# A mixture-of-experts step on 32-column quarters of TensorE, with the hidden layer turned on VectorE

## The chip, the cores and the metric

The kernel runs on one core of a Trainium2 chip. The metric is the device time of one execution in microseconds (us), from the first to the last instruction. A core has five engines that run side by side: TensorE (PE) multiplies matrices, VectorE (DVE) and ScalarE (ACT) work elementwise, GpSimd (POOL) and SyncE (SP) here mostly start transfers between the chip's main memory and the core's own memory (SBUF). TensorE takes two operands from SBUF: one (`lhsT`, the stationary one) is loaded into its array first, the other (`rhs`, the moving one) streams through. The result lands in PSUM, whence ScalarE or VectorE fetch it.

## The reference: attention, a router, and one expert for each token

All is in float32. Attention within chunks of 64 positions gives 4608 token rows of 512 values. A router picks one of 8 experts for each row by cosine similarity. The expert is a two-layer network, 512 to 1024 to 512, whose result is scaled by the router's weight. Cut to what matters:

```python
# q, k, v: (8, 8, 576, 64); w1: (8, 512, 1024); w2: (8, 1024, 512)
x = chunk_attention(q, k, v)                  # (4608, 512), chunks of 64
logits = normalize(x) @ normalize(expert_emb).T / tau
expert_idx = np.argmax(logits, axis=1)
gate_w = softmax(logits)[np.arange(N), expert_idx]
for e in range(E):
    mask = expert_idx == e
    h = np.maximum(x[mask] @ w1[e], 0.0)      # first layer, ReLU
    out[mask] = gate_w[mask, None] * (h @ w2[e])   # second layer
```

## The kernel before

The kernel has two stages. The first computes attention and the router, writes the token rows to main memory and sorts them by expert into groups of up to 64 rows. The second takes two groups at a time, so 128 rows are one step (`j`), and each half of the step (`s`) has its own expert's weights. There are 37 steps. 36 of them (`LEAST`) are in a software pipeline; the last one stands alone behind a branch (`more`), since the number of steps depends on the data. The names are `P = 128`, `G = 64`, `D = 512`, `F = 1024`, `KD = D / P = 4`, `KF = F / P = 8`.

A step has these parts. `turn_xb` turns the step's 128 rows on TensorE (a product with the identity), so that the 512 inputs lie on the partitions. `gates` works out the router's weights on ScalarE and VectorE. `hidden` is the first layer, `turn_h` turns its result, and `result` is the second layer:

```python
def hidden(j):
    d = mo[j]
    h = bp.tile([P, F], FP32, tag="h", name="h")
    for fh in range(F // 512):
        ps = ps_h.tile([P, 512], FP32, tag="h", name="h_ps")
        for c in range(KD):
            for s in range(2):
                nc.tensor.matmul(
                    ps[G * s : G * s + G],
                    lhsT=d["xT"][:, c, G * s : G * s + G],
                    rhs=w1_sb[s][j % 2][:, c, fh * 512 : fh * 512 + 512],
                    start=(c == 0), stop=(c == KD - 1),
                )
        dst = h[:, fh * 512 : fh * 512 + 512]
        if fh % 2:
            nc.scalar.activation(dst, ps, AF.Relu)
        else:
            nc.vector.tensor_scalar(dst, ps, 0.0, None, ALU.max)
    d["h"] = h

def turn_h(j):
    d = mo[j]
    hT = bp.tile([P, KF, P], FP32, tag="hT", name="hT")      # two buffers
    for g in range(KF // 4):
        ps = ps_ht.tile([P, 4, P], FP32, tag="ht", name="ht_ps")
        for c in range(4):
            f0 = (4 * g + c) * P
            nc.tensor.transpose(ps[:, c], d["h"][:, f0 : f0 + P], ident)
        if g % 2:
            nc.scalar.copy(hT[:, 4 * g : 4 * g + 4], ps)
        else:
            nc.vector.tensor_copy(hT[:, 4 * g : 4 * g + 4], ps)
    d["hT"] = hT

def result(j):
    d = mo.pop(j)
    ps = ps_y.tile([P, D], FP32, tag="y", name="y_ps")
    for c in range(KF):
        for s in range(2):
            nc.tensor.matmul(
                ps[G * s : G * s + G],
                lhsT=d["hT"][:, c, G * s : G * s + G],
                rhs=w2_sb[s][j % 2][:, c],
                start=(c == 0), stop=(c == KF - 1),
            )
    y = bp.tile([P, D], FP32, tag="y", name="y", bufs=3)
    nc.scalar.activation(y, ps, AF.Copy, scale=d["gate"])
    # ... (the rows of y are sent to their places in the output)
```

A matmul whose result lies on 64 of the 128 partitions uses 64 of the array's 128 columns; the two halves `s` of a step use the two halves of the array in turn. The order of the parts in the loop:

```python
for j in range(LEAST + 1):
    if j + 1 < LEAST:
        hidden(j + 1)
        # ... load_w1(j + 3): weights, only where the expert changes
    if j < LEAST:
        turn_h(j)
    if j + 2 < LEAST:
        turn_xb(j + 2)
        gates(j + 2)
    if j > 0:
        result(j - 1)
        # ... load_w2(j + 1)
    # ... (rows for later steps are gathered)
# ... more(LEAST): the last step, its parts one after the other
```

In the first stage, the attention scores (`sc`) are also matmuls on parts of the array: tiles of 64 rows by 64 columns, four of them in turn, 16 matmuls for each 128 rows.

Of the kernel before, what the change touches and what calls it, by code (L numbers as in the profile page):

```python
# [9 lines left out]
FP32 = mybir.dt.float32  # L10
BF16 = mybir.dt.bfloat16
I32 = mybir.dt.int32
AF = mybir.ActivationFunctionType
ALU = mybir.AluOpType
AX = mybir.AxisListType
PSUM = bass.MemoryType.PSUM
ENG = mybir.EngineType

P = 128
# [6 lines left out]
def kernel(  # L26
# [11 lines left out]
    nc = tc.nc  # L38
    B, H, S, Dh = q.shape
    E, D = moe_expert_emb.shape  # L40
    F = moe_w1.shape[2]
    N = B * S
    NPAIR = H // 2
    KD = D // P
    KF = F // P
    NT = N // P
    NCB = S // CH
    G = P // 2
    NST = NT + E // 2
    scale = 1.0 / float(Dh) ** 0.5  # L50
    XBUF = 4
# [13 lines left out]
    w1_sb = [[keep.tile([P, KD, F], FP32, name=f"w1_{s}{i}") for i in range(2)] for s in range(2)]  # L65
    w2_sb = [[keep.tile([P, KF, D], FP32, name=f"w2_{s}0")] for s in range(2)]
    w1_rows = moe_w1.rearrange("e (c p) f -> p (e c) f", p=P)
    w2_rows = moe_w2.rearrange("e (c p) d -> p (e c) d", p=P)
    ident = keep.tile([P, P], FP32, name="ident")
# [492 lines left out]

    with (
        tc.tile_pool(name="blk", bufs=2) as bp,
        tc.tile_pool(name="ps_x", bufs=1, space=PSUM) as ps_x,
        tc.tile_pool(name="ps_h", bufs=3, space=PSUM) as ps_h,
        tc.tile_pool(name="ps_ht", bufs=2, space=PSUM) as ps_ht,
        tc.tile_pool(name="ps_y", bufs=2, space=PSUM) as ps_y,
    ):
        def number(ap, top, *engines):  # L570
            return nc.values_load(
                ap,
                engines=engines,
                min_val=0,
                max_val=top,
                skip_runtime_bounds_check_because="a count of comparisons, less than this",
            )

        new = {}

        def load_w(buf, rows, n, s, j):

            if (s, j) not in new:
                new[s, j] = (
                    number(eblk[G * s : G * s + 1, j : j + 1], E - 1, ENG.SP),
                    number(fresh[G * s : G * s + 1, j : j + 1], 1, ENG.SP),
                )
            e, f = new[s, j]
            nc.sync.dma_start(out=buf[s][j % 2], in_=rows[:, ds(e * n, n), :], cond=f > 0)

        def load_w1(j):
            for s in range(2):
                load_w(w1_sb, w1_rows, KD, s, j)

        def load_w2(j):
            for s in range(2):
                load_w(w2_sb, w2_rows, KF, s, j)
                del new[s, j]

        def turn_xb(j):  # L600
            t = xin.pop(j)
            ps = ps_x.tile([P, KD, P], FP32, tag="x", name="x_ps")
            for c in range(KD):
                nc.tensor.transpose(ps[:, c], t[:, c * P : c * P + P], ident)  # L604
            xT = bp.tile([P, KD, P], FP32, tag="xbT", name="xbT")
            nc.vector.tensor_copy(xT, ps)
            mo[j] = {"xT": xT, "xin": t}

        def gates(j):
            d = mo[j]  # L610
            x, lg = d["xin"], spot[:, j, 0:E]
            junk = bp.tile([P, D], FP32, tag="junk", name="junk", bufs=1)
            rn = bp.tile([P, 1], FP32, tag="rn", name="rn")
            lmax = bp.tile([P, 1], FP32, tag="lmax", name="lmax")
            sh = bp.tile([P, E], FP32, tag="sh", name="sh")
            gate = bp.tile([P, 1], FP32, tag="gate", name="gate", bufs=4)
            nc.scalar.activation(junk, x, AF.Square, accum_out=rn)
            nc.scalar.activation(rn, rn, AF.Sqrt)  # L618
            nc.vector.tensor_reduce(lmax, lg, axis=AX.X, op=ALU.max)
            nc.vector.tensor_scalar(rn, rn, 1e-6, None, ALU.add)  # L620
            nc.vector.reciprocal(rn, rn)
            nc.vector.tensor_scalar(sh, lg, lmax, rn, ALU.subtract, ALU.mult)
            nc.scalar.activation(sh, sh, AF.Exp, accum_out=gate)  # L623
            nc.vector.tensor_scalar(gate, gate, 1e-9, None, ALU.add)
            nc.vector.reciprocal(gate, gate)
            d["gate"] = gate

        def hidden(j):
            d = mo[j]
            h = bp.tile([P, F], FP32, tag="h", name="h")  # L630
            for fh in range(F // 512):
                ps = ps_h.tile([P, 512], FP32, tag="h", name="h_ps")
                for c in range(KD):
                    for s in range(2):
                        nc.tensor.matmul(  # L635
                            ps[G * s : G * s + G],
                            lhsT=d["xT"][:, c, G * s : G * s + G],
                            rhs=w1_sb[s][j % 2][:, c, fh * 512 : fh * 512 + 512],
                            start=(c == 0),
                            stop=(c == KD - 1),  # L640
                        )
                dst = h[:, fh * 512 : fh * 512 + 512]
                if fh % 2:
                    nc.scalar.activation(dst, ps, AF.Relu)  # L644
                else:
                    nc.vector.tensor_scalar(dst, ps, 0.0, None, ALU.max)  # L646
            d["h"] = h

        def turn_h(j):
            d = mo[j]  # L650
            hT = bp.tile([P, KF, P], FP32, tag="hT", name="hT")
            for g in range(KF // 4):
                ps = ps_ht.tile([P, 4, P], FP32, tag="ht", name="ht_ps")
                for c in range(4):
                    f0 = (4 * g + c) * P
                    nc.tensor.transpose(ps[:, c], d["h"][:, f0 : f0 + P], ident)  # L656
                if g % 2:
                    nc.scalar.copy(hT[:, 4 * g : 4 * g + 4], ps)
                else:
                    nc.vector.tensor_copy(hT[:, 4 * g : 4 * g + 4], ps)  # L660
            d["hT"] = hT

        def result(j):
            d = mo.pop(j)
            ps = ps_y.tile([P, D], FP32, tag="y", name="y_ps")
            for c in range(KF):
                for s in range(2):
                    nc.tensor.matmul(  # L668
                        ps[G * s : G * s + G],
                        lhsT=d["hT"][:, c, G * s : G * s + G],  # L670
                        rhs=w2_sb[s][j % 2][:, c],
                        start=(c == 0),
                        stop=(c == KF - 1),
                    )
            y = bp.tile([P, D], FP32, tag="y", name="y", bufs=3)
            nc.scalar.activation(y, ps, AF.Copy, scale=d["gate"])  # L676
            ins = nc.gpsimd.indirect_dma_start(  # L677
                out=out,
                out_offset=bass.IndirectOffsetOnAxis(ap=spot[:, j, E : E + 1].bitcast(I32), axis=0),
                in_=y,  # L680
                in_offset=None,
                bounds_check=N - 1,
                oob_is_err=False,
            )
            tc.declare_no_dep(ins.ins, group="rows", reason="blocks hold different tokens")
            tc.add_to_no_dep_group("rows", ins.ins)

        load_w1(0)
        load_w1(1)
        load_w2(0)  # L690
        load_w2(1)
        turn_xb(0)
        hidden(0)
        load_w1(2)
        gates(0)
        turn_xb(1)
        gates(1)

        LEAST = NT
        for j in range(LEAST + 1):  # L700
            if j + 1 < LEAST:
                hidden(j + 1)
                if j + 3 < NST:
                    load_w1(j + 3)
            if j < LEAST:
                turn_h(j)
            if j + 2 < LEAST:
                turn_xb(j + 2)
                gates(j + 2)
            if j > 0:  # L710
                result(j - 1)
                if j + 1 < NST:
                    load_w2(j + 1)
            if j + XBUF < NST:
                gather_x(j + XBUF)
                if j + XBUF + 1 < NST:
                    gather_spot(j + XBUF + 1)

        steps = number(n_steps, NST, ENG.PE, ENG.DVE, ENG.Activation, ENG.Pool, ENG.SP)

        def more(j):
            with tc.If(steps > j):
                turn_xb(j)
                hidden(j)
                if j + 2 < NST:
                    load_w1(j + 2)
                turn_h(j)
                gates(j)
                result(j)
                if j + 2 < NST:  # L730
                    load_w2(j + 2)
                if j + 1 < NST:
                    more(j + 1)

        more(LEAST)


# [26 lines left out]
```

## Time and profile before

| | before |
|---|---|
| median of 3 runs | 804.73 us (802.67 to 807.33) |
| profiled execution | 810.2 us |
| TensorE matmuls busy | 743.9 us (92%) |
| TensorE weight loads busy | 367.7 us (45%) |
| VectorE busy | 251.7 us (31%) |
| ScalarE busy | 290.7 us (36%) |
| mean of transfers | 163 GB/s |

In the profile a matmul instruction in float32 appears as two records, each with a record of a weight load (LDWEIGHTS) before it. A line of a group gives the line of the source, the engine, the operation, what it writes and reads, the part of the array (128\*64 is 128 rows by 64 columns), the shape and the number of records, then the busy time in us and the mean length of a record in ns, and last the engine's idle time ahead of it with what ended that. Records of matmuls overlap, so a mean length is more than a record's share of the time. The chain of waits follows the work back from the last instruction, at each step to what released it. The page's rows of digits cut the span into 40 equal slices, and a digit is the busy share in tenths. In the tables by windows the busy times are in the order PE, PE weight loads, VectorE, ScalarE, GpSimd, then the share of TensorE's full clock that was granted, the share of the transfer engines' time, and GB/s.

### The profile page before, as it was taken

The numbers are of one execution on the slowest core, as the hardware profiler recorded it, in microseconds if no ns is written. First come the engines' busy times: TensorE is split into PE (matmuls) and PEld (weight loads), VectorE is DVE, ScalarE is ACT, GpSimd is POOL, SyncE is SP. The second block draws the span as 40 slices with busy tenths as digits, with TensorE's granted clock in tenths as the row PEclk, the third lists the DMA queues.
The fourth block names the chain that finished last, engine by engine and source line by source line (L and its number), as shares of the span: only waits on it lengthen the run. The fifth ranks groups of instructions, "written<-read, shape, count | busy, mean of one in ns | idle before, by whom it ended". The sixth has DMA issues, their size and how long they took to land.

```text
span 810.2 us, 15342 instructions
## 1 busy us (share of the span) xinstructions
PE 743.9 (92%) x6033; PEld 367.7 (45%) x6033; DVE 251.7 (31%) x703; ACT 290.7 (36%) x520; POOL 221.3 (27%) x270
## 2 busy tenths in 40 slices
PE   2799999985569999999999999999999999999994
PEld 2688888874124333343343333343333343333331
DVE  2467777775221121121121121121121122122100
ACT  3345455441142243243243243333334334334102
POOL 4235556545420211211211311311211221221220
PEclk9999999995778999999999999999999999999998
DMA  9999999993670100115583416688530444312140
GB/s 177 234 264 246 238 251 234 258 399 133 233 247 1 51 27 27 53 59 202 189 305 131 155 61 229 253 328 323 169 118 27 144 144 131 140 44 79 72 150 9
DMA packets 117739, 132.37 MB, mean 163 GB/s; under 512 B 79860, under 2 KB 83252, under 8 KB 117664
## 3 DMA queue, kind: packets, MB, share of 16 engines
q1 hardware_dynamic: 101136, 84.18, 35.9%
q0 software_dynamic: 16528, 47.17, 18.4%
q8 instruction: 49, 0.80, 0.4%
q14 instruction: 26, 0.21, 0.1%
HBM read 383.07 MB, written 21.80 MB: 500 GB/s over the span
## 4 chain that ended last, share of the span: by engine, by line
PE 83%; DMA 4%; issue 3%; DVE 3%; SPq 3%; POOL 1%; ACT 0%; POOLq 0%; DVEq 0%; ACTq 0%
PE y_ps L668 31%; PE h_ps L635 29%; PE ht_ps L656 4%; PE rt_ps L288 4%; PE pv L255 3%; PE tr L280 3%; PE tr L199 3%; PE sc L215 2%; SPq L188 2%; PE tr L241 2%; PE x_ps L604 2%; DMA w<-in_moe_w_dram 2%; DMA spot<-spots,src_row 1%; DVE x L266 1%; SPq L176 1%
## 5 line engine op out<-in xcount | busy, mean ns | idle before, releaser
L635 PE MATMUL h_ps<-w,xbT 128*64 128x512 f32 x1184 | 267.9, 604 | 9.9 <-DMA w<-in_moe_w_dram 6.6
L668 PE MATMUL y_ps<-w,hT 128*64 128x512 f32 x1184 | 262.0, 595 | 0.0
L635 PEld LDWEIGHTS h_ps<-w,xbT 128*64 128x64 f32 x1184 | 88.5, 140 | 181.3 <-issue 174.4
L677 POOL DMA_INDIRECT out_dram<-y,spot x37 | 37.8, 1022 | 441.6 <-ACT y L676 425.7
L668 PEld LDWEIGHTS y_ps<-w,hT 128*64 128x64 f32 x1184 | 81.8, 137 | 154.6 <-issue 154.1
L644 ACT ACTIVATE h<-h_ps 128x512 f32<-128x512 f32 x37 | 22.1, 597 | 259.2 <-PE h_ps L635 231.8
L646 DVE TENSOR_SCALAR h<-h_ps 128x512 f32<-128x512 f32 x37 | 25.6, 691 | 225.4 <-PE h_ps L635 225.4
L676 ACT ACTIVATE y<-y_ps,gate 128x512 f32<-128x512 f32 x37 | 25.4, 687 | 126.1 <-PE y_ps L668 126.1
L660 DVE COPY hT<-ht_ps 128x512 f32<-128x512 f32 x37 | 25.6, 692 | 126.9 <-PE ht_ps L656 123.5
L623 ACT ACT_TABLE_LOAD x37 | 47.5, 1283 | 0.7
L618 ACT ACT_TABLE_LOAD x37 | 47.5, 1283 | 0.7
L527 POOL DMA_INDIRECT xin<-x_rows,spot x40 | 41.4, 1034 | 22.2 <-issue 11.3
L656 PEld LDWEIGHTS ht_ps<-ident,h 128*128 128x128 f32 x296 | 31.7, 141 | 30.4 <-issue 29.2
L282 ACT COPY xT<-tr 128x512 f32<-128x512 f32 x36 | 21.1, 586 | 64.8 <-PE tr L280 46.1
L527 POOL DMA_INDIRECT spot<-spots,src_row x40 | 40.4, 1009 | 13.9 <-issue 11.6
L288 PE MATMUL rt_ps<-enT,xT 128*128 128x8 f32 x288 | 37.6, 257 | 5.8 <-DVE m L310 5.7
L199 PE MATMUL tr<-ident,kx 128*128 128x128 f32 x144 | 24.2, 296 | 18.4 <-DMA kx<-in_k_dram 18.4
L288 PEld LDWEIGHTS rt_ps<-enT,xT 128*128 128x128 f32 x288 | 37.5, 203 | 7.7 <-DVE m L310 4.1
L656 PE MATMUL ht_ps<-ident,h 128*128 128x128 f32 x296 | 40.6, 280 | 0.1
L176 POOL DMA_DIRECT2D qx<-in_q_dram x40 | 35.3, 886 | 19.0 <-PE tr L199 17.8
L372 POOL DMA_INDIRECT spots<-m,dest x36 | 36.7, 1019 | 11.4 <-issue 10.6
L273 POOL DMA_DIRECT2D x_rows<-x x36 | 20.3, 565 | 70.0 <-DVE x L266 55.8
(123 smaller groups left out, 659.3 us busy)
## 6 DMA issues: line engine op xcount, KB each, us to landing
w<-in_moe_w_dram SPq DMA_DIRECT2D x160, 2048.0 KB
v<-in_v_dram SPq DMA_DIRECT2D x64, 144.0 KB
x_rows<-x POOLq DMA_DIRECT2D x36, 256.0 KB
qx<-in_q_dram POOLq DMA_DIRECT2D x32, 256.0 KB
kx<-in_k_dram SPq DMA_DIRECT2D x32, 256.0 KB
w<-in_moe_w_dram POOLq DMA_DIRECT2D x4, 2048.0 KB
spots<-empty SPq DMA_DIRECT2D x1, 2312.0 KB
qx<-in_q_dram POOLq DMA_DIRECT2D x8, 128.0 KB
```

The costliest lines, as they stand in the source:

```text
L176: eng.dma_start(out=x[done : done + n], in_=src[b, :, s : s + n, :].rearrange("h p d -> p h d"),)
L199: nc.tensor.transpose(ps[:, i], a[:, i * P : i * P + P], ident)
L288: nc.tensor.matmul(rt_ps[:, 0, batch_of[t][1]], lhsT=d["xT"][:, c], rhs=enT[:, c], start=(c == 0), stop=(c == KD - 1),)
L372: ins = nc.gpsimd.indirect_dma_start(out=spots, out_offset=bass.IndirectOffsetOnAxis(ap=at, axis=0), in_=m, in_offset=None, bounds_check=S ...
L527: nc.gpsimd.indirect_dma_start(out=dst, out_offset=None, in_=table, in_offset=bass.IndirectOffsetOnAxis(ap=at, axis=0), bounds_check=rows - 1,
L618: nc.scalar.activation(rn, rn, AF.Sqrt)
L623: nc.scalar.activation(sh, sh, AF.Exp, accum_out=gate)
L635: nc.tensor.matmul(ps[G * s : G * s + G], lhsT=d["xT"][:, c, G * s : G * s + G], rhs=w1_sb[s][j % 2][:, c, fh * 512 : fh * 512 + 512], sta ...
L646: nc.vector.tensor_scalar(dst, ps, 0.0, None, ALU.max)
L656: nc.tensor.transpose(ps[:, c], d["h"][:, f0 : f0 + P], ident)
L668: nc.tensor.matmul(ps[G * s : G * s + G], lhsT=d["hT"][:, c, G * s : G * s + G], rhs=w2_sb[s][j % 2][:, c], start=(c == 0), stop=(c == KF ...
L677: ins = nc.gpsimd.indirect_dma_start(out=out, out_offset=bass.IndirectOffsetOnAxis(ap=spot[:, j, E : E + 1].bitcast(I32), axis=0), in_=y, ...
```

## The change

The change does away with turning h on TensorE. VectorE can turn squares of 32x32 between SBUF and SBUF. So that turned squares are all that is needed, the first layer is computed in quarters of 32 array columns: quarter `r` gets 32 token rows on its 32 partitions, and of the 1024 hidden columns those that lie at places `32 r` to `32 r + 31` in each block of 128. A square turned within its partitions `32 r` to `32 r + 31` is then already where the second layer wants it. ScalarE applies the ReLU, VectorE turns, and the turned result lies in one of three buffers instead of two. The second layer is in quarters too. The PSUM that the turning of h used goes to the first layer (four buffers instead of three) and to the turning of x (two instead of one).

```diff
+    Q = 32
...
-        tc.tile_pool(name="ps_x", bufs=1, space=PSUM) as ps_x,
-        tc.tile_pool(name="ps_h", bufs=3, space=PSUM) as ps_h,
-        tc.tile_pool(name="ps_ht", bufs=2, space=PSUM) as ps_ht,
+        tc.tile_pool(name="ps_x", bufs=2, space=PSUM) as ps_x,
+        tc.tile_pool(name="ps_h", bufs=4, space=PSUM) as ps_h,
...
         def hidden(j):
             d = mo[j]
-            ... (the body above, and turn_h)
+            hT = bp.tile([P, KF, P], FP32, tag="hT", name="hT", bufs=3)
+            for s in range(2):
+                w = w1_sb[s][j % 2].rearrange("p c (k r i) -> p c r k i", r=P // Q, i=Q)
+                ps = ps_h.tile([P, G // Q, KF * Q], FP32, tag="h", name="h_ps")
+                for b in range(G // Q):
+                    t0 = G * s + Q * b
+                    for c in range(KD):
+                        for r in range(P // Q):
+                            nc.tensor.matmul(
+                                ps[Q * r : Q * r + Q, b].rearrange("p (k i) -> p k i", i=Q),
+                                lhsT=d["xT"][:, c, t0 : t0 + Q],
+                                rhs=w[:, c, r],
+                                start=(c == 0),
+                                stop=(c == KD - 1),
+                            )
+                h = bp.tile([P, G // Q, KF * Q], FP32, tag="h", name="h")
+                nc.scalar.activation(h, ps, AF.Relu)
+                nc.vector.transpose(
+                    hT[:, :, G * s : G * s + G].rearrange("p k (b i) -> p b k i", i=Q),
+                    h.rearrange("p b (k i) -> p b k i", i=Q),
+                )
             d["hT"] = hT
...
             for c in range(KF):
-                for s in range(2):
+                for r in range(P // Q):
                     nc.tensor.matmul(
-                        ps[G * s : G * s + G],
-                        lhsT=d["hT"][:, c, G * s : G * s + G],
-                        rhs=w2_sb[s][j % 2][:, c],
+                        ps[Q * r : Q * r + Q],
+                        lhsT=d["hT"][:, c, Q * r : Q * r + Q],
+                        rhs=w2_sb[r // 2][j % 2][:, c],
...
-            if j < LEAST:
-                turn_h(j)
...
-                turn_h(j)
```

The last two cuts are in the loop and in `more`. `turn_xb`, `gates`, the loads of weights and the gathering of rows stay as they are.

More of the change, by code (lines that the diff above doesn't have):

```diff
@@ L629, in hidden @@
             d = mo[j]
[L630 to L633, printed above, removed]
-                    for s in range(2):
-                        nc.tensor.matmul(
-                            ps[G * s : G * s + G],
[L637 to L660, printed above, removed]
+            hT = bp.tile([P, KF, P], FP32, tag="hT", name="hT", bufs=3)
@@ L666, in result @@
             for c in range(KF):
-                for s in range(2):
+                for r in range(P // Q):
                     nc.tensor.matmul(
-                        ps[G * s : G * s + G],
-                        lhsT=d["hT"][:, c, G * s : G * s + G],
-                        rhs=w2_sb[s][j % 2][:, c],
+                        ps[Q * r : Q * r + Q],
+                        lhsT=d["hT"][:, c, Q * r : Q * r + Q],
+                        rhs=w2_sb[r // 2][j % 2][:, c],
                         start=(c == 0),
```

## The prediction

> **What bounds the kernel now.** I read the page's first two parts, then the chain of waits over one expert step, then the groups by cost, then busy times in windows. First the page: shares of the span, and the 40 slices of about 20 us.
>
> ```profile
> span 810.2 us, 15342 instructions
> ...
> PE 743.9 (92%) x6033; PEld 367.7 (45%) x6033; DVE 251.7 (31%) x703; ACT 290.7 (36%) x520; POOL 221.3 (27%) x270
> ...
> PE   2799999985569999999999999999999999999994
> ...
> PEclk9999999995778999999999999999999999999998
> ```
>
> From slice 14 (about 260 us) to the last slice TensorE is never idle, at full clock. The chain of waits between 506 and 530 us shows who sets the pace in there (columns: start, length, what, records):
>
> ```profile
> 506.33 6.87 PE h_ps L635 x32
> 513.20 1.02 PE ht_ps L656 x8
> 514.22 0.44 PE x_ps L604 x4
> 514.66 7.02 PE y_ps L668 x32
> 521.67 6.87 PE h_ps L635 x32
> ```
>
> The chain is TensorE alone, without a gap. One expert step (128 token rows) takes 521.67 - 506.33 = 15.34 us: first layer 6.87, turning h 1.02, turning the next x 0.44, second layer 7.02. The 64 layer records of a step take 13.89 us, 217 ns each. The groups say what else the h turning costs:
>
> ```profile
> L656 PE MATMUL ht_ps<-ident,h 128*128 128x128 f32 x296 | 40.6, 280 | 0.1
> ...
> L644 ACT ACTIVATE h<-h_ps 128x512 f32<-128x512 f32 x37 | 22.1, 597 | 259.2 <-PE h_ps L635 231.8
> L646 DVE TENSOR_SCALAR h<-h_ps 128x512 f32<-128x512 f32 x37 | 25.6, 691 | 225.4 <-PE h_ps L635 225.4
> ...
> L660 DVE COPY hT<-ht_ps 128x512 f32<-128x512 f32 x37 | 25.6, 692 | 126.9 <-PE ht_ps L656 123.5
> ```
>
> x296 over 37 steps is 8 turning records a step. The copies on ScalarE and VectorE mostly wait for TensorE (the last column), so their own time costs nothing. The table by windows confirms it for one step: TensorE busy 15.34 of 15.34, VectorE 3.07, ScalarE 5.56.
>
> ```profile
> 268.50:283.84 15.34, 15.34 (x78) 5.80 (x77) 3.07 (x10) 5.56 (x10) 3.06 (x3) 1.00 0.11 37
> ```
>
> **What the Trainium skill says.** (1) "TensorEngine Tiling (Array Packing)", Tiling Modes: with all 128 rows the array can be two tiles of 64 columns or four of 32, tiles work in parallel, and changing the mode drains the engine. The trace agrees for two: a record of one 64-column half lasts 604 ns (mean), yet one starts every 215 ns in the first layer (6.87/32), so two run at once. No run here shows four tiles of 32 columns. (2) "TensorE: Matmul & The Clock Gate", Part 3: three column tiles of 32 gave a measured 2.38 times, against an ideal 3, for one isolated pack; its section on LDWEIGHTS says a load takes time by its columns, about P/1.2 ns. The trace agrees: in the router stage (119.56 us in the chain) a record with 128 loaded and only 8 moving columns takes 0.79/8 = 99 ns, near P/1.2 = 107, so there the load sets the pace. (3) "VectorE: DVE Perf Modes", The three transpose paths: VectorE turns only blocks of 32x32, to SBUF. That is why the layer must be in quarters: quarter r holds columns r*32 to r*32+31 of every block of 128, so turned squares land on their right partitions. (4) "FP8 and Floating Point Precision": true fp32 is four passes. The trace has two records for each fp32 matmul (1184 over 37 steps is 32, for 16 matmuls), two passes each, so I count records.
>
> **The change, part by part.**
>
> *First layer.* Before: 16 matmuls of 512 columns, 32 records in two halves. After: 2 groups x 2 blocks x 4 chunks x 4 quarters = 64 matmuls of 256 columns, 128 records in four quarters. Array work is the same: 16 x 512 / 2 = 4096 column times, 64 x 256 / 4 = 4096. If four quarters run as well as two halves, a record starts every 6.87/128 = 54 ns. A load of 32 columns in the background is then needed every 54 ns; by P/1.2 that is 27 ns (an estimate from the page in (2)), so it fits even if loads go one after another. Can TensorE start records this fast? The score matmuls of the attention stage, in four 64x64 tiles, say yes:
>
> ```profile
> 120.36 0.62 PE sc L215 x32
> ```
>
> 0.62/32 = 19 ns a record, each with its weight load. The extra cost of starting: a half now gets a new record every 6.87/16 = 429 ns, against 427 for two passes of 512 columns at the 2.4 GHz of the page in (2), so some 2 ns for each turn of a half. Each quarter has 32 turns in place of each half's 16, so +16 x 2 = +0.03 us. First layer: 6.90 us.
>
> *Second layer.* Before 16 matmuls, after 8 x 4 = 32, all of 512 columns: 64 records, 4 at once, 107 ns apart. The same 7.02 us.
>
> *Turning h.* The 8 records go: -1.02 us. But not all of that is work. The x turning, same shape, takes 0.44/4 = 110 ns a record, so eight are 0.88; the other 0.14 is the change from half mode to whole mode, which now falls to the x turning, since 128x32 to 128x128 and back is still done once a step. Net -0.88.
>
> *ScalarE and VectorE.* ScalarE loses a copy (585 ns) and gets a second ReLU (597 ns): no change. VectorE loses a ReLU (691) and a copy (692), and gets two transposes of 512 elements for each partition; I take some 0.7 us each, by the copies' 692 ns for the same count. All this beside TensorE.
>
> *The new way round.* h no longer goes to TensorE and back. hT of step j+1 is written while the second layer reads j-1, with j waiting: that is what three buffers are for. From the end of a first layer to its hT: ReLU 0.6 + transpose 0.7 = 1.3 us, with one whole step of slack. No wait in the loop.
>
> *Sum.* A step: 6.90 + (0.44 + 0.14) + 7.02 = 14.50 us, against 15.34: -0.84. It counts in 35 steps. The first turning (at 234 us) lies in a wait for second-layer weights that ends at about 242 us whatever TensorE does, so it pays nothing. In step 37, which is alone behind a branch, second-layer work starts 1.5 us after the first layer's end (790.0 to 791.5 us), and ReLU + transpose take about as long. So -0.84 x 35 = -29.4 us: 804.7 - 29.4 = 775.3 us.
>
> **The rivals.**
>
> *Four quarters cost more than two halves.* They read four moving streams at once, in the first layer in runs of 32 elements at steps of 128, and load weights four times as often. For it: no four-column mode in the trace, and the skill's 2.38 of 3 for one pack. Against: a long stream hides the fill that a single pack shows, as the halves do (427 of 429 ns), and the score matmuls start at 19 ns. If the first layer alone lost 10%, that is 0.7 x 37 = +26: about 801 us. If both lost 10%, 37 x 1.4 = +52: 827, slower than before. Break-even is at 0.84/13.9 = 6% on both layers, so the whole gain hangs on this.
>
> *The round through ScalarE and VectorE becomes a wait.* If TensorE had to stop for ReLU and transpose each step, 1.3 us would replace 0.84: 36 x 0.46 = +17, about 821 us. Against: the three buffers, VectorE's 3.07 busy of 15.34, and the order of instructions, which puts a second layer and a first layer between the write and the read. Even a transpose of 2 us would be hidden.
>
> *The weights come late.* Between 536 and 562 us transfers run at about 400 GB/s without pause. A shorter step asks for them 0.84 us earlier for each step. TensorE did not wait there before. The burst beginning at 537 us ends at 563, the second-layer weights asked for at 552 are wanted at about 576: over 10 us to spare. Worth +5 us at worst.
>
> **Range and chances.** The best case, all 1.02 gone with no added start cost, is -36 us: 769. A loss of up to 5% in the first layer alone (0.35 x 37 = 13) gives 788. I put about 0.8 on 767 to 802, with a tail above for the first rival. Faster by over 2% is below 788.6: 0.80. Within 2%: 0.08. Slower: 0.12. Point: 775.5.
>
> **What would show it.** Right: first-layer records 54 ns apart, a step of 14.5 us in the chain, ht_ps gone, x_ps at about 0.58, two VectorE transposes of about 0.7 us a step, TensorE busy all through a step. Wrong: h_ps well over 6.9 us or y_ps well over 7.02 (the quarters don't run at full rate); gaps before y_ps put down to VectorE (the second rival) or before h_ps or y_ps put down to a transfer (the third). The prediction falls if a layer in quarters takes over 7.4 us.

## The result, and the profile after

The changed kernel takes 774.94 us (median; 772.02 to 781.06), the kernel before 805.14 us. The ratio is 0.9636, with a 95% interval of 0.9571 to 0.9700. The prediction was 775.5 us, with a range of 767 to 802.

The page of the changed kernel, in the parts that were shown of before:

```profile
span 770.1 us, 24290 instructions
...
PE 705.6 (92%) x10473; PEld 390.4 (51%) x10473; DVE 249.0 (32%) x703; ACT 289.7 (38%) x520; POOL 221.6 (29%) x270
...
PE   2699999995558999999999999999999999999993
...
PEclk9899999996688999999999999999999999999998
```

TensorE is still the engine that never rests in the expert stage; the 40 slices are only shorter, 19.3 us each in place of 20.3. The number of instructions went up by 8948, as quarters need more matmuls and loads, and the time went down all the same. The chain of waits over one expert step (start, length, what, records):

```profile
518.00 0.59 PE x_ps L604 x4
518.59 7.00 PE y_ps L661 x64
525.59 6.91 PE h_ps L641 x128
532.50 0.59 PE x_ps L604 x4
```

A step is now 532.50 - 518.00 = 14.50 us: first layer 6.91, turning x 0.59, second layer 7.00. Nothing but TensorE is on the chain, and the turning of h is gone from it. The groups show where it went:

```profile
L641 PE MATMUL h_ps<-w,xbT 128*32 128x256 f32 x4736 | 267.2, 384 | 12.2 <-DMA w<-in_moe_w_dram 7.2
...
L650 DVE STREAM_TRANSPOSE hT<-h 128x512 f32<-128x512 f32 x74 | 52.7, 712 | 353.3 <-ACT h L649 353.3
```

The first layer's 4736 records are busy for 267.2 us, where the 1184 of before were busy for 267.9. VectorE's 74 transposes take 712 ns each, and VectorE idles ahead of them (353.3 us in all) until ScalarE has done the ReLU, so they have time to spare.

A caution on spans. The two profiled executions differ by 810.2 - 770.1 = 40.1 us, more than the medians' 30.2. The chain shows a first layer starting at 242.24 us before and at 233.68 us after, right behind the wait for weights: 8.6 us of the 40 lie ahead of it, and the attention code there is the same in both. In the profiles of the experiments the corresponding point lies between 232.0 and 242.7 us, but for the two runs whose first layer is itself much slower. What the change does is read from the step, 0.84 us shorter.

### The profile page after: what moved, and what is told of

It reads as the page before. It is cut to its first block, busy times and chain, and to the rows that moved or that the text cites. A ratio compares the mean times of both kernels' runs of the same rounds, so it can differ in the third digit from the quotient of the medians.

```text
span 770.1 us, 24290 instructions
## 1 busy us (share of the span) xinstructions
PE 705.6 (92%) x10473; PEld 390.4 (51%) x10473; DVE 249.0 (32%) x703; ACT 289.7 (38%) x520; POOL 221.6 (29%) x270
## 3 DMA queue, kind: packets, MB, share of 16 engines
q0 software_dynamic: 16528, 47.17, 19.3%
## 4 chain that ended last, share of the span: by engine, by line
PE 83%; DMA 6%; DVE 3%; issue 3%; SPq 2%; POOL 1%; ACT 0%; POOLq 0%; DVEq 0%
PE y_ps L661 33%; PE h_ps L641 31%; PE rt_ps L289 4%; PE tr L200 3%; PE sc L216 3%; PE x_ps L604 3%; PE pv L256 2%; PE tr L242 2%; PE tr L281 2%; DMA kx<-in_k_dram 2%; DMA w<-in_moe_w_dram 2%; DMA spot<-spots,src_row 1%; SPq L189 1%; DVE mx L224 1%; DVE a L226 1%
## 5 line engine op out<-in xcount | busy, mean ns | idle before, releaser
L641 PE MATMUL h_ps<-w,xbT 128*32 128x256 f32 x4736 | 267.2, 384 | 12.2 <-DMA w<-in_moe_w_dram 7.2
L661 PE MATMUL y_ps<-w,hT 128*32 128x512 f32 x2368 | 262.3, 594 | 0.7 <-DVE lmax L619 0.7
L641 PEld LDWEIGHTS h_ps<-w,xbT 128*32 128x32 f32 x4736 | 154.9, 111 | 131.7 <-issue 32.2
L650 DVE STREAM_TRANSPOSE hT<-h 128x512 f32<-128x512 f32 x74 | 52.7, 712 | 353.3 <-ACT h L649 353.3
L661 PEld LDWEIGHTS y_ps<-w,hT 128*32 128x32 f32 x2368 | 73.7, 110 | 163.6 <-issue 161.7
L670 POOL DMA_INDIRECT out_dram<-y,spot x37 | 37.9, 1024 | 409.8 <-ACT y L669 393.8
L649 ACT ACTIVATE h<-h_ps 128x512 f32<-128x512 f32 x74 | 44.2, 598 | 236.5 <-PE h_ps L641 236.5
L604 PE MATMUL x_ps<-ident,xin 128*128 128x128 f32 x148 | 24.7, 291 | 12.7 <-DMA xin<-x_rows,spot 12.7
L606 DVE COPY xbT<-x_ps 128x512 f32<-128x512 f32 x37 | 24.2, 655 | 24.0 <-PE x_ps L604 24.0
L205 DVE COPY qxT<-tr 128x512 f32<-128x512 f32 x36 | 24.7, 687 | 21.1 <-PE tr L200 19.3
```

Source lines behind the costliest of these rows:

```text
L641: nc.tensor.matmul(ps[Q * r : Q * r + Q, b].rearrange("p (k i) -> p k i", i=Q), lhsT=d["xT"][:, c, t0 : t0 + Q], rhs=w[:, c, r], start=(c ...
L649: nc.scalar.activation(h, ps, AF.Relu)
L650: nc.vector.transpose(hT[:, :, G * s : G * s + G].rearrange("p k (b i) -> p b k i", i=Q), h.rearrange("p b (k i) -> p b k i", i=Q),)
L661: nc.tensor.matmul(ps[Q * r : Q * r + Q], lhsT=d["hT"][:, c, Q * r : Q * r + Q], rhs=w2_sb[r // 2][j % 2][:, c], start=(c == 0), stop=(c = ...
L670: ins = nc.gpsimd.indirect_dma_start(out=out, out_offset=bass.IndirectOffsetOnAxis(ap=spot[:, j, E : E + 1].bitcast(I32), axis=0), in_=y, ...
```

## The experiments

The theory is the prediction's: the gain is TensorE's time for eight turnings, less the mode change that passes to the x turning, while the quarters cost and bring nothing. The first rival is that quarters run at another rate than halves. The first two runs cross the two parts of the change.

**Halves, with VectorE turning.** From the kernel before:

```diff
-                    nc.tensor.transpose(ps[:, c], d["h"][:, f0 : f0 + P], ident)   # and the copies
+                nc.vector.transpose(hT[:, 4 * g : 4 * g + 4].rearrange("p k i -> p (k i)"),
+                                    d["h"][:, 512 * g : 512 * g + 512])   # hT in three buffers
```

> Both layers stay in halves of the array as before, but h is turned in 32x32 squares on VectorE into one of three buffers, and the eight turnings on TensorE are left out. In halves the squares do not land where the second layer wants them, so this leaves out a part of the turning and the result is not the reference's; its time tells what turning off TensorE is worth without quarters. Theory (quarters cost and bring nothing, the gain is the eight turning records less the mode change that passes to the x turning): a step of 6.87 + 0.58 + 7.02 = 14.47 us, 774 us in all, the same as the changed kernel. Rival (quarters are themselves faster or slower than halves): this kernel differs from the changed one by over 1%.

The transposes stand right behind the first layer here, and PSUM is divided as in the changed kernel. Measured: 771.9 us, ratio 0.9601 (0.9569 to 0.9633). The chain over a step:

```profile
521.14 0.59 PE x_ps L603 x4
521.72 7.02 PE y_ps L663 x32
528.74 6.87 PE h_ps L634 x32
```

The step is 14.47 us, as expected: the x turning has grown from 0.44 to 0.59 here too, without any quarter. So that growth is the mode change which the h turning had carried.

**Quarters, with TensorE turning.** From the changed kernel, the transposes on VectorE are replaced by `turn_h` of before.

> Both layers in quarters as in the changed kernel, but h is turned on TensorE again, eight turnings a step, with the copies and PSUM buffers of before. h lies in quarters, so these turnings do not give the second layer what it wants and the result is not the reference's. Theory: a step of 6.91 + 1.02 + 0.44 + 7.00 = 15.37 us, about 805 us, the same as before. Rival (quarters bring a part of the gain): below 795 us; (quarters cost): above 815.

Measured: 804.15 us, ratio 1.0005 (0.9981 to 1.0029). Chain:

```profile
506.53 6.91 PE h_ps L642 x128
513.44 1.02 PE ht_ps L663 x8
514.46 0.44 PE x_ps L605 x4
514.90 7.00 PE y_ps L675 x64
```

The quarters alone change nothing: 15.37 us a step against 15.34. The two runs together put the whole gain on the turning; quarters are only what makes VectorE's squares land in the right place. The division of PSUM went with the turning in both runs, so they don't part the two; but in the chain of before each stretch of TensorE's work follows the last without a gap, so there was no wait for a PSUM buffer to take away.

**Second layer in halves.** From the changed kernel:

```diff
-                for r in range(P // Q):    # ps[Q * r : ...], hT[:, c, Q * r : ...], w2_sb[r // 2]
+                for s in range(2):         # ps[G * s : ...], hT[:, c, G * s : ...], w2_sb[s]
```

> The changed kernel with the second layer in halves again; the result stays the reference's. Theory (a change of the array's mode costs TensorE some 0.1 to 0.15 us, and quarters as such nothing): from the second layer to the next first layer there is now one more change, +0.12 us a step, about 14.62 us a step and 779 us. Rival (quarters in the second layer cost something): faster than 775 us; (a change of mode costs nothing): 775 us.

Measured: 781.11 us, ratio 0.9702 (0.9670 to 0.9735). Chain:

```profile
517.70 7.04 PE h_ps L641 x128
524.75 0.59 PE x_ps L604 x4
525.34 7.02 PE y_ps L661 x32
```

The first layer, whose code is untouched, takes 7.04 in place of 6.91 us, because the array now changes from halves to quarters ahead of it. The step is 14.65 us, +0.15. This is why both layers are in quarters: with halves in the second the result would be right too, at a cost of some 5 us (35 x 0.15).

**Two buffers for the turned h.** From the changed kernel:

```diff
-            hT = bp.tile([P, KF, P], FP32, tag="hT", name="hT", bufs=3)
+            hT = bp.tile([P, KF, P], FP32, tag="hT", name="hT", bufs=2)
```

> The changed kernel with two buffers for the turned h in place of three. Theory (the third buffer is needed for VectorE's order): the turning of step j+1 then has to wait until the second layer of step j-1 has been read out; VectorE works in order, so the copy of the turned x that the next first layer needs stands behind the two turnings, and TensorE waits some 2 x 0.71 + 0.65 + 0.2 = 2.3 us ahead of each first layer: a step of 16.8 us, about 855 us. Rival (the third buffer is a comfort, since a turned h is wanted only a step later): 775 us.

Measured: 856.44 us, ratio 1.0682 (1.0642 to 1.0722). The chain, and VectorE in order of time in the same step (start, length, instruction, idle before and its releaser):

```profile
531.52 7.00 PE y_ps L661 x64
538.52 2.15 issue
```

```profile
538.69 1.30 DVE L650 STREAM_TRANSPOSE hT<-h 128x512 f32<-128x512 f32 x2 [15.28 <-PE y_ps L661]
539.92 0.65 DVE L606 COPY xbT<-x_ps 128x512 f32<-128x512 f32 x1
```

VectorE stands for 15.28 us until the second layer (`y_ps`) has read the old buffer, then turns twice, and only then copies the x that the next first layer waits for: 1.30 + 0.65 and the ends, the 2.15 us of the chain. Note that the chain calls this "issue"; only VectorE's own timeline tells what it was. The first layer behind the wait takes 7.11 us in place of 6.91, so the step is 16.85 us, +2.35. Three of these first layers take some 1.65 us more, because the granted clock stands at half for 3.4 us (0.51 from 522.14 to 525.50 us); it stands at full in the other steps from 250 us on, and what sets these three apart is not shown.

Is it VectorE's order, or are two buffers too few? In a first run x is copied by ScalarE, which is not held up.

```diff
-            nc.vector.tensor_copy(xT, ps)
+            nc.scalar.copy(xT, ps)        # and hT with bufs=2
```

> Two buffers for the turned h, as in the run that lost 82 us, but the turned x is copied by ScalarE in place of VectorE; the result stays the reference's. Theory (the loss was VectorE's order: the copy of x that the next first layer waits for stood behind two turnings that could not start): TensorE waits no more, a step of 14.5 us, 775 us. Rival (two buffers are too few for the turned h itself): still over 840 us.

Measured: 820.74 us against 813.39 of before on that chip, ratio 1.0084 (1.0048 to 1.0120). Neither expected figure came. TensorE in order of time:

```profile
519.93 7.07 PE L661 MATMUL y_ps<-w,hT 128*32 128x512 f32 x64
526.82 8.20 PE L641 MATMUL h_ps<-w,xbT 128*32 128x256 f32 x128
534.95 0.66 PE L604 MATMUL x_ps<-ident,xin 128*128 128x128 f32 x4
```

The wait ahead of the first layer is gone, as the theory said, but the first layer itself now takes 8.1 us. The loads of weights in this first layer show that its last records come in small groups; between them stands the first of three instructions by which GpSimd moves rows:

```profile
526.82 6.58 PEld L641 LDWEIGHTS h_ps<-w,xbT 128*32 128x32 f32 x118 [0.30 <-issue]
530.29 1.02 POOL L670 DMA_INDIRECT out_dram<-y,spot  x1 [12.17 <-ACT y L669]
533.88 0.17 PEld L641 LDWEIGHTS h_ps<-w,xbT 128*32 128x32 f32 x6 [0.48 <-issue]
```

Two more runs take this apart. One keeps two buffers and only moves the transposes behind the second layer in VectorE's order:

```diff
             if j > 0:
                 result(j - 1)
+            if j + 1 < LEAST:
+                turn_h(j + 1)     # the two nc.vector.transpose, taken out of hidden; bufs=2
```

> Two buffers for the turned h again, but the two transposes of step j+1 are put into VectorE's order behind the second layer of step j-1 (and so behind the copy of the turned x and the router's weights), where their buffer is free anyway; ScalarE and VectorE have the work of the changed kernel, and the result stays the reference's. Theory (the loss with two buffers was only the order on VectorE): 775 us, a ratio of 0.963, with no wait ahead of the first layer. Rival (two buffers are too few by themselves, which the slower first layers of the run with ScalarE's copy leave possible): over 810 us.

Measured: 773.66 us, ratio 0.9624 (0.9576 to 0.9673): as fast as three buffers. The other keeps three buffers and lets ScalarE copy x:

```diff
-            nc.vector.tensor_copy(xT, ps)
+            nc.scalar.copy(xT, ps)        # hT with bufs=3
```

> The changed kernel, with its three buffers, and only the turned x copied by ScalarE in place of VectorE; the result stays the reference's. It is to tell where the first layers of 8.2 to 8.4 us came from in the run with two buffers and ScalarE's copy. If from the two buffers, with VectorE standing still in front of its turnings: 775 us here, a ratio of 0.963 and first layers of 6.9 us. If from the copy on ScalarE: first layers of over 8 us and a ratio above 1.0.

Measured: 772.35 us, ratio 0.9644 (0.9575 to 0.9713). So neither two buffers nor ScalarE's copy cost anything by themselves; what costs is a VectorE that stands still in front of its transposes. By which way it slows the first layer when x no longer depends on it stays open: the trace puts nothing but "issue" ahead of the late records. There is a candidate. Behind the transposes VectorE also holds back the router's weights, so ScalarE scales `y` late, and GpSimd's three row instructions begin 3.47 us into each first layer, where they begin 1.24 us into it in the changed kernel and in the last two runs. The small groups come from 7.0 us into the layer on, where the three end (7.1 us). But in the changed kernel the same three leave no gap, and no run moves them alone, so that they hold TensorE up is not shown; the next run has a similar coincidence.

**How far are the quarters from their limit?** Each first-layer matmul cut into four:

```diff
+                    for u in range(4):    # around the loops over c and r
-                                rhs=w[:, c, r],
+                                    rhs=w[:, c, r, 2 * u : 2 * u + 2],   # 64 columns
```

> The changed kernel with each first-layer matmul of 256 columns cut into four of 64, so four times the matmuls and weight loads for the same array work (512 records a step instead of 128, 13 ns of array work each); the result stays the reference's. It asks how near the 54 ns a record of the changed kernel is to the pace at which quarters can be loaded and started. If loads of different quarters run side by side and only starting counts, a record each 19 ns as in the score matmuls of the attention stage: a first layer of 9.7 us, a step of 17.3 us, about 876 us. If loads of the four quarters go one after another, 27 to 29 ns each: a first layer of 14.3 us, a step of 21.9 us, about 1040 us; then the 54 ns had less than half to spare. If the limit lies at 54 ns or near: 27 us a first layer, over 1400 us.

Measured: 1119.42 us against 813.39, ratio 1.3758 (1.3710 to 1.3805). None of the three figures. The end of one first layer in the chain:

```profile
540.41 1.99 PE h_ps L642 x128
542.40 1.75 issue
544.16 1.14 PE h_ps L642 x65
```

While records come, 128 of them take 1.99 us, 15.5 ns each, each with its load. So loads of different quarters do run side by side, faster than the 27 ns that one after another would need by the prediction's estimate, and the changed kernel's 54 ns has far more than half to spare. The time is lost in between, in two kinds of stops. The packets of instructions on TensorE's queue, in the changed kernel and here (packets, MB, share):

```profile
q8 instruction: 85, 1.39, 0.7%
...
q8 instruction: 196, 3.21, 1.2%
```

Cutting the matmuls added 28416 records on TensorE (matmuls and loads) and 111 packets of 16384 bytes. That is 256 records a packet and 64 bytes each, the size of an instruction that the Trainium skill gives ("Perfetto Trace Analysis", The 4-stage abstract model). The first kind of stop, some 130 us in all, follows these packets: 39 times in the loop TensorE runs exactly 256 records from one stop to the next, 128 matmul records with their loads, and every time it goes on 1.25 to 1.58 us after a packet has landed. No run changed the supply, so that TensorE waits for its instructions rests on this count and timing.

The second kind, some 120 us in all, stands between small groups, four to six records with their loads, 0.75 us from group to group. In all 32 regular steps of the loop the first such group comes 0.54 to 0.59 us behind the first of GpSimd's three row instructions, and in the two steps where those came 0.8 us later, so did the groups. This is a coincidence in time, not a cause shown. Besides, the granted clock stood at half in 35 stretches of the loop, 130 us together, and never in the changed kernel's loop, so a part of the loss is clock.

**The form of the moving operand.** Two runs change only which columns a quarter reads:

```diff
-                w = ....rearrange("p c (k r i) -> p c r k i", r=P // Q, i=Q)   # runs of 32
+                w = ....rearrange("p c (k i r) -> p c r k i", r=P // Q, i=Q)   # every fourth column
```

> The changed kernel with the moving weights of the first layer read as every fourth column instead of runs of 32 columns: quarter r takes columns r, r+4, r+8 and so on of each block of 128. The hidden columns then lie in another order than the second layer takes them in, so the result is not the reference's; the work is the same. Theory (TensorE's moving operand costs the same in runs of 32 elements as contiguous, and the form of the run was no part of the time): with 16 bytes from one element to the next I expect the rate to suffer, if at all, only here: 775 us if a record stays at 54 ns. Rival (short runs cost): a first layer of 10 us or more, over 880 us.

Measured: 1053.03 us against 813.39, ratio 1.2954 (1.2909 to 1.3000). The first layer in the chain:

```profile
515.38 14.49 PE h_ps L641 x127
```

```diff
+                w = ....rearrange("p c (m r u) -> p c r m u", r=P // Q, u=4)   # runs of four
```

> The changed kernel with the moving weights of the first layer read in runs of four columns, 16 bytes each, 64 bytes apart, between the runs of 32 of the changed kernel (7.0 us a first layer) and the single columns, 16 bytes apart, that took 14.5 us. The hidden columns lie in another order than the second layer takes them in, so the result is not the reference's. If what costs is each new 16 bytes for one element, the first layer is back at 6.9 us and the ratio at 0.963. If a run has to be longer, it lies between 7 and 14.5 us.

Measured: 772.95 us, ratio 0.9608 (0.9573 to 0.9642). The first layer in the chain:

```profile
512.24 6.91 PE h_ps L641 x128
```

Single columns 16 bytes apart cost 113 ns a record, runs of four (16 bytes) 54. The Trainium skill's "SBUF — State Buffer", Door 1, says that full bandwidth needs at least two hits to a line of 16 bytes; both runs agree. The rival in the single-column run was right: the form counts. It makes no difference between runs of four and the 32 of the change.

**Turning x in pairs.** If a mode change costs 0.15 us, half of them can go. From the changed kernel:

```diff
-            if j + 2 < LEAST:
-                turn_xb(j + 2)
-                gates(j + 2)
+            if j % 2 == 0:
+                for i in (j + 2, j + 3):
+                    if i < LEAST:
+                        turn_xb(i)
+            if j + XBUF < NST:
+                gather_x(j + XBUF)      # taken from the end of the loop
+            if j + 2 < LEAST:
+                gates(j + 2)
```

> The changed kernel with the turning of x done for two steps at a time, in every second step, and the gathering of x moved ahead of the second layer; the result stays the reference's. Theory (each change of the array's mode costs, by the chain of the changed kernel: the x turning takes 0.59 us next to 0.44 without a change ahead of it, and the second layer 7.00 next to 6.91 for the first, so 0.24 us for the pair): half of these changes go, -0.12 us a step, 35 steps, -4 us: about 771 us. Rival (a change of mode costs nothing of its own): the same time as the changed kernel. Other rival (x is not there yet when two are turned at once): slower.

> The changed kernel once more, beside the kernel with x turned in pairs: 775 us, a ratio of 0.963 to the kernel before.

Measured on the same chip: 769.46 us, ratio 0.9545 (0.9506 to 0.9584), and the changed kernel again 774.72 us, ratio 0.9607 (0.9570 to 0.9644). The chain over two steps:

```profile
518.32 1.02 PE x_ps L604 x8
519.34 7.00 PE y_ps L661 x64
526.35 6.91 PE h_ps L641 x128
533.25 6.87 PE y_ps L661 x64
540.12 6.91 PE h_ps L641 x128
547.03 1.02 PE x_ps L604 x8
```

Two steps take 28.71 us instead of 29.00. The second layer behind a first layer takes 6.87, behind an x turning 7.00: this change of mode is 0.13 us. The one into the x turning is 0.14 to 0.15 us (1.02 for two turnings and 0.59 for one, with 0.44 of work each). The gain is 0.145 us a step; the medians differ by 5.3 us, and the two intervals overlap a little, so the step in the chain is the better evidence. The gathering of x was moved as well, but the chain has no wait in either kernel that this could have taken away. Nothing of the work is left out, and no other such kernel here has a lower median.

## Why the prediction was right

*First layer, 6.90 us:* 6.91 in the chain. The records come 54 ns apart. *Second layer, 7.02:* 7.00. *Turning h, net -0.88:* the crossed runs confirm both halves of this term, the 1.02 us that goes and the 0.14 that stays with the x turning (0.44 to 0.59). Taking the plain 1.02 would have promised 5 us too much (35 x 0.14).

*The step, 14.50:* 14.50. That it fits to the last digit is luck: the first layer and the x turning came 0.01 us longer than predicted, the second layer 0.02 shorter. *35 steps, -29.4 us:* the medians say -30.2. What was left out held too, though one reading was wrong: the wait that swallows the first turning is for weights of the first layer (`h_ps` waits 6.6 us there before), not of the second. Whichever it was, the turning lay inside it. In the last step the second layer's main part starts 8.52 us after the first layer's start before (783.02 to 791.54) and 8.62 after (742.94 to 751.56), so the way over ScalarE and VectorE is worth the same as the turning there.

Another reading was loose: records of 604 ns that start 215 ns apart would make nearly three at once, not two, as a record's length is more than its share of the array. The sum used only the starts.

*ScalarE and VectorE:* transposes 712 ns, against some 0.7 us. *No wait in the loop:* right, but the reason given was only half of it. The prediction put it down to the three buffers giving a step of slack. The run with transposes placed later shows that two buffers do as well; the third is needed because the transposes stand, in VectorE's order, ahead of work that TensorE waits for.

*First rival, quarters at another rate:* false, by the crossed runs. The guard against loads that go one after another, 27 ns each, was not needed: a record with its load took 15.5 ns in the cut matmuls. *Second rival, the round becomes a wait:* false; neither the changed kernel nor the one with two buffers has a gap ahead of the second layer in the chain of the loop. What two buffers bring is another wait, which the prediction did not think of: it stands ahead of the first layer, for the copy of x behind the transposes, and costs 2.15 us a step where the rival had 1.3. *Third, late weights:* false; the groups show 7.2 us of waiting for weights on the first layer (6.6 before), which is at the stage's start, and the chain has none in the loop.

## What to carry to other kernels

Where one engine is busy all through a stage, price a change by that engine's instructions in the chain, and ask for each removed group which overhead it carried for its neighbours. Work that is moved to an idle engine is free only if the instructions behind it on that engine don't have to wait for its buffers; place it behind them, or give it another buffer. Cutting TensorE's work into column quarters was free here with moving runs of 16 bytes (four columns) and of 32 columns, and with some 400 TensorE instructions in a step of 14.5 us; it was not with single columns, nor with some 1160 instructions a step.

## What was not expected

Single float32 columns 16 bytes apart halve the rate of the moving operand (113 against 54 ns a record), and four in a row restore it. Quarter-array records start 15.5 ns apart with their loads, but a first layer of 512 of them is held up by stops, often of about 2 us, that come after exactly 256 records and end 1.25 to 1.58 us after a packet of instructions lands. And a VectorE that stands still slowed TensorE's first layers (8.1 instead of 6.91 us) though their own input no longer waited for it; how, is open, and GpSimd's later row instructions are the candidate.
